# A two-mixture kernel: weight statistics two experts ahead, rows of conditional blocks turned inside the main block, two low parts per expert on GpSimd

## The chip, the cores and the metric

The kernel runs on one core of one Trainium2 chip. The metric is the device time of one execution in microseconds (us); lower is better. Engines are called PE (TensorE matmul), PEld (its weight load), DVE (VectorE), ACT (ScalarE), POOL (GpSimd) and SP (SyncE, which issues most of the transfers).

## The reference

Three layers follow one another on 2304 tokens of width 512: attention inside chunks of 64, a mixture of 8 experts where each token goes to one expert, and a second mixture where each token goes through all 8 experts. Only the first mixture is touched by the change:

```python
logits = x @ w_gate
expert_idx = np.argmax(logits, axis=1)
...
gate_w = probs[np.arange(N), expert_idx]
...
h = np.maximum(np.einsum('ecd,edf->ecf', disp, w1), 0.0)
y = np.einsum('ecf,efd->ecd', h, w2)
...
        out[i] = gate_w[i] * y[expert_idx[i], pos[i]]
```

`disp` holds, for each expert, the tokens that chose it. An expert has a first layer of 512 to 1024 and a second of 1024 to 512, in float32.

## The kernel before

Every float32 matrix is scaled by a power of two and split into two float16 parts, a high one and a low one (the remainder). A product is then three float16 products: high by high, high by low, low by high. The scale of a weight matrix comes from a statistic of the whole matrix.

**Weights of the first mixture.** Expert x has matrix "a" (first layer) and "b" (second). `loads(x, nm)` brings one in as four transfers of 512 KB on SP's queue, into a staging buffer that expert x and expert x + 2 share. `w_stat` takes the statistic of a quarter: for "a" a sum of squares on ACT (line 157), for "b" a maximum on DVE (line 159). `w_scale` adds the quarters up over the partitions with a small PE product, `w_scale2` makes the scale on DVE in some ten tiny operations. `w_split` makes the parts of a quarter: the high part on ACT (line 217), the low part on DVE (line 218) as scale times the staged weights minus the high part. A variant with `on_pool` scales in place on DVE first and subtracts on POOL (line 215); it is used for expert 0 alone, during the attention.

**Tokens of an expert.** `gather` fetches 128 rows at a time by an indirect transfer on POOL's queue (line 652) into one of six `xg` buffers. `turn_dma` transposes the first 256 rows of the next expert by transfers on SP's queue. `turn` transposes on PE instead (line 673): eight 128 by 128 transposes for each 128 rows into a PSUM bank, then one copy on ACT and one on DVE (lines 675 and 676).

**An expert's turn in the loop over x.** `blocks(..., main=True)` computes the first 256 tokens: the first layer in four groups of 24 products (line 705), each followed by `hh` (relu and high part, ACT, line 709) and `hl` (low part, DVE, line 710); then for each 128 tokens t the second layer in 24 products (line 720), its sum of squares on ACT, a scale on DVE, the two halves of the output row (lines 729 and 730) and `rkt`, the token number and the gate factor (lines 735 and 736). The `hh` and `hl` of the main block use PSUM banks "p" (three), the second layer banks "y" (two), the conditional blocks banks "c" (two). Then come the conditional blocks: if the expert has more than 256 tokens, one block of 128, if more than 384, one of 256. With this data experts 0 and 2 run a block of 256, experts 3 and 6 one of 128, experts 1, 4, 5 and 7 none. The rows for the conditional block are `late`; before the change they are turned on PE at the start of the conditional block.

**The order around it.** Each engine takes its instructions in program order. Work on the weights of the next expert y = x + 1 is put into `sites`, six places of the main block of x: after each of the four groups and after each of the two second layers. Before the change the first three sites hold the statistics of y, the fourth its scales and two splits, the fifth four splits, the sixth two. Loads for expert x + 3 follow the main block. Expert 7's sites prepare the first matrix of the second mixture (`w_quad`: sums of sub-blocks on POOL, lines 233 to 236, then parts on ACT and DVE, lines 242 and 243). After the loop the second mixture begins at line 916 with products that read rows already written.

Of the kernel before, what the change touches and what calls it, by code (L numbers as in the profile page):

```python
# [10 lines left out]
F16 = mybir.dt.float16  # L11
# [20 lines left out]
def kernel(ctx, tc, q, k, v, w_gate, w1, w2, capacity, w2_gate, w21, w22, out):  # L32
    nc = tc.nc
# [34 lines left out]
    def sm(nm, shape, dtype=F32):  # L68
        return small_pool[-1].tile(shape, dtype, tag=nm, name=nm)
# [135 lines left out]
        n = 2 * ((x - E) % 2) if x >= E else 2 * (nm == "b")  # L205
        m.hi, m.lo = (w_slot(x, n + i).rearrange("p (k n) -> p k n", n=m.n) for i in range(2))

    def w_split(x, nm, j, nj, on_pool=False):
        m = mats[x, nm]
        c = m.kk // nj  # L210
        sl = slice(j * c, (j + 1) * c)
        if on_pool:
            nc.vector.tensor_scalar(out=m.st[:, sl, :], in0=m.st[:, sl, :], scalar1=m.s, scalar2=None, op0=ALU.mult)
            nc.scalar.copy(out=m.hi[:, sl, :], in_=m.st[:, sl, :])
            nc.gpsimd.tensor_tensor(out=m.lo[:, sl, :], in0=m.st[:, sl, :], in1=m.hi[:, sl, :], op=ALU.subtract)
        else:
            nc.scalar.activation(out=m.hi[:, sl, :], in_=m.st[:, sl, :], func=AF.Copy, scale=m.s)  # L217
            nc.vector.scalar_tensor_tensor(out=m.lo[:, sl, :], in0=m.st[:, sl, :], scalar=m.s, in1=m.hi[:, sl, :],  # L218
                                           op0=ALU.mult, op1=ALU.subtract)
# [44 lines left out]
    with ExitStack() as actx:  # L264
# [310 lines left out]
        def plan(n, f):  # L575
            todo.setdefault(n, []).append(f)

        for nm, ld, st, sc, sp in (("a", (2, 3), (3, 4, 5, 6), 6, (10, 13, 8, 15)), ("b", (9, 10), (11, 10, 12, 12), 12, (15, 14, 16, 13))):
            for h in range(2):
                plan(ld[h], lambda nm=nm, h=h: w_load(0, nm, h))  # L580
                plan(NT + 1, lambda nm=nm, h=h: w_load(1, nm, h))
            for h in range(4):
                plan(st[h], lambda nm=nm, h=h: w_stat(0, nm, h, True))
            plan(sc, lambda nm=nm: (w_scale(0, nm), w_alloc(0, nm)))
            plan(sc + 1, lambda nm=nm: w_scale2(0, nm))
            for h in range(4):
                plan(sp[h], lambda nm=nm, h=h: w_split(0, nm, h, 4, True))

        order = ((st_x1, 4), (st_scale, 5), (st_exp, 3), (st_lo, 6), (st_scores, 2), (st_hi, 5), (st_norm, 4), (st_xtr, 4),
                 (st_max, 2), (st_xcopy, 4), (st_tr, 0), (st_pv, 3), (st_logits, 5), (st_dtr, 2))  # L590
# [46 lines left out]
    with ExitStack() as cctx:  # L637
# [24 lines left out]
            return xT, rows  # L662


        def turn(rows, main):
            if main:
                xT = cp.tile([128, 2 * KD, 256], F16, tag="xT", name="xT", bufs=2)
            else:
                xT = cp.tile([128, 2 * KD, 256], F16, tag="xTc", name="xTc", bufs=1)
            for n, (idx, kg, xg) in enumerate(rows):  # L670
                p = ps_c.tile([128, 2 * KD, 128], F16, tag="y" if main else "c", name="p_t", bufs=2)
                for kk in range(2 * KD):
                    nc.tensor.transpose(p[:, kk, :], xg[:, kk * 128:(kk + 1) * 128], id16)
                sl = slice(n * 128, (n + 1) * 128)
                nc.scalar.copy(out=xT[:, 0:KD, sl], in_=p[:, 0:KD])
                nc.vector.tensor_copy(xT[:, KD:2 * KD, sl], p[:, KD:2 * KD])
            return xT, rows

        def blocks(x, pre, nb, row0, sites=(), main=False):
            a, b = mats[x, "a"], mats[x, "b"]
            xT, rows = pre
            W = 128 * nb
# [2 lines left out]
            def bank(nm, shape):  # L687
                tag, bufs = {"p": ("p", 3), "y": ("y", 2)}[nm] if main else ("c", 2)
                return ps_c.tile(shape, F32, tag=tag, name="p_" + nm, bufs=bufs)

            def site():
                for f in (sites.pop(0) if sites else ()):
                    f()

            hh = cp.tile([128, KF, 256], F16, tag="hh", name="hh", bufs=1)[:, :, 0:W]
            hl = cp.tile([128, KF, 256], F16, tag="hl", name="hl", bufs=1)[:, :, 0:W]
            FG = 512 // W
# [15 lines left out]
            for t in range(nb):  # L713
                idx, kg, _ = rows[t]
                sl = slice(t * 128, t * 128 + 128)
                y = bank("y", [128, DM])
                n = 0
                for kk in range(KF):
                    for h, w in ((hh, b.hi), (hh, b.lo), (hl, b.hi)):
                        nc.tensor.matmul(y, lhsT=h[:, kk, sl], rhs=w[:, kk, :], start=(n == 0), stop=(n == 3 * KF - 1))  # L720
                        n += 1
                sq, ssq = cp.tile([128, DM], BF16, tag="sq", name="sq2", bufs=1), sm("ssq2", [128, 1])
                nc.scalar.activation(out=sq, in_=y, func=AF.Square, accum_out=ssq)
                s, inv = sm("x2s", [128, 1]), sm("x2i", [128, 1])
# [9 lines left out]
                to = sm("rkt", [128, 2])  # L734
                nc.gpsimd.tensor_copy(to[:, 1:2].bitcast(I32), idx)
# [12 lines left out]
        def scales(x):  # L748
            return [lambda f=f, nm=nm: f(x, nm) for f in (w_scale, w_scale2) for nm in "ab"]

        def loads(x, nm, lo=0, hi=4):
            for h in range(lo, hi):
# [19 lines left out]
        late = gather(tokens(0, 2, 3))  # L772
        for f in stats(1):
            f()
        pre = turn(first, True)

        for x in range(E):
            y = x + 1
# [17 lines left out]
            if x == E - 1:  # L796
                with tc.If(rc <= 512):
                    heads()
            if y < E:
                for nm in "ab":  # L800
                    w_alloc(y, nm)
                steps = [stats(y) if x > 0 else []] + [scales(y) + each(w_split, y, "a", 4, 4) + each(w_split, y, "b", 4, 4)]
                counts = (4, 2, 2), (6, 4, 2)
            else:
                w_alloc(E, "a")
                wsums += [xw.tile([128, 4, 2, 128], F32, name=f"wsum{i}") for i in range(2)]
                quads = lambda *qs: [lambda q=q, i=i: w_quad(E, q, i) for q, i in qs]
                steps = [quads((0, 0), (1, 0)) + stats(E),
                         scales(E) + quads((0, 1), (0, 2), (2, 0), (1, 1), (1, 2), (3, 0), (2, 1), (2, 2), (3, 1), (3, 2))]
                counts = (6, 2, 2), (6, 5, 3)  # L810
            sites = []
            for fs, ns in zip(steps, counts):
                for n in ns:
                    sites.append(fs[:n])
                    fs = fs[n:]
                assert not fs
            blocks(x, cur, 2, ranks(0), sites, True)
            if x + 3 < E + 1:
                for nm in "ab":
                    if (x + 3, nm) != (E, "b"):  # L820
                        loads(x + 3, nm)
            if x == E - 2:
                loads(E, "b")
            with tc.If(rc > 256):
                with tc.If(rc > 384) as cmp:
                    blocks(x, turn(late, False), 2, ranks(2))
                    with tc.If(rc > 512):
                        with tc.For_i(4, (rc + 127) // 128, 1) as t:
                            idx = cp.tile([128, 1], I32, tag="idx", name="idx")
                            nc.vector.tensor_copy(idx, gidx[:, x, bass.ds(t, 1)])  # L830
                            blocks(x, turn(gather([idx]), False), 1, lambda _: rank(t))
                        if x == E - 1:
                            heads()
                with cmp.Else():
                    blocks(x, turn(late[:1], False), 1, ranks(2))

    w_alloc(E, "b")
    acctx.close()
# [255 lines left out]
    for x in range(E):  # L1094
# [27 lines left out]
        if x < 2:  # L1122
            for i, f in sq.items():
                if (i >= 34) == (x == 1):
                    plan(2 * (1 - x), i - 34 * x, f)
        if x == 0:
            for h in range(4):
                plan(0, 2 * h + 5, lambda h=h: w_split(E, "b", h, 4))
        for s in range(NSB):
# [73 lines left out]
```

## Time and profile before

| what | us |
|---|---|
| median of 3 runs (1909.0 to 1911.2) | 1910.93 |
| the profiled execution | 1911.24 |
| its span, first to last instruction | 1909.2 |
| the first mixture in it, from the first product of expert 0 (152.49) to the first of the second mixture (455.50) | 303.01 |
| PE busy in this stretch | 254.10 |

The profiled execution lasts 2.04 us longer than its span. Everything that the change edits lies between 152.49 and some microseconds after 455.50.

### The profile page before, as it was taken

To read this page: it belongs to the slowest core of one execution; us is meant where nothing else is said; L and a number is where in the kernel's file an instruction comes from. 1 tells how busy PE (TensorE), PEld (TensorE's weight loads), DVE (VectorE), ACT (ScalarE), POOL (GpSimd) and SP (SyncE) were. 2 spreads that over 40 slices of the span, in tenths; PEclk is the share of its full clock that TensorE was granted. 3 is DMA by queue.
4 is the path that set the end of the run, shared out by engine and by line. 5 is a ranking of instruction groups with operands and counts; after the bars stand their busy time and mean duration, and the time that the engine had idled before them with its cause. 6 is when DMAs were issued, how large, how long until landed. Compare 5 with 4: busy or idle time off the path is not lost.

```text
span 1909.2 us, 27168 instructions
## 1 busy us (share of the span) xinstructions
PE 1789.2 (94%) x10671; PEld 1013.1 (53%) x10671; DVE 1019.8 (53%) x1981; ACT 717.0 (38%) x1300; POOL 404.7 (21%) x470
## 2 busy tenths in 40 slices
PE   6867988888998999999999999999999999999998
PEld 5755645556554445555555555555555555555553
DVE  4894545757656554453555346444535553464432
ACT  7953544646433333332333224322323332242210
POOL 2341101113111211130133014111311230042221
PEclk8987989989999999999999999999999999999999
DMA  9745465754412211121122021311211211212210
GB/s 227 194 156 189 103 231 140 168 152 124 136 42 102 94 59 59 54 93 58 59 102 86 17 102 59 102 59 45 102 59 59 102 67 36 103 58 70 73 42 33
DMA packets 135119, 182.14 MB, mean 95 GB/s; under 512 B 62240, under 2 KB 80752, under 8 KB 134960
## 3 DMA queue, kind: packets, MB, share of 16 engines
q1 hardware_dynamic: 128544, 162.75, 27.3%
q0 software_dynamic: 5360, 17.24, 3.2%
q8 instruction: 100, 1.64, 0.4%
q14 instruction: 59, 0.48, 0.1%
q10 hardware_dynamic: 1056, 0.03, 0.0%
HBM read 149.21 MB, written 23.56 MB: 90 GB/s over the span
## 4 chain that ended last, share of the span: by engine, by line
PE 68%; DVE 4%; ACT 3%; issue 1%; POOL 1%; DMA 0%; POOLq 0%; DVEq 0%
PE p_m L1088 39%; PE p_m L1026 28%; DVE c L1032 1%; DVE el L1043 1%; ACT eh L1042 1%; ACT wsq L157 1%; POOL w L1061 1%; PE p_m L916 0%; PE p_l L166 0%; ACT m L1051 0%; ACT m L1071 0%; DVE w L218 0%; DVE u L1032 0%; ACT w L217 0%; DMA out_dram<-acc,rk 0%
## 5 line engine op out<-in xcount | busy, mean ns | idle before, releaser
L1088 PE MATMUL p_m<-w,eh 128*128 128x512 f16 x2304 | 685.2, 379 | 0.6 <-ACT eh L1042 0.6
L1026 PE MATMUL p_m<-x,w 128*128 128x384 f16 x4032 | 667.6, 327 | 1.3 <-DVE c L1032 1.3
L1026 PEld LDWEIGHTS <-w 128*128 128x128 f16 x4032 | 396.2, 99 | 264.9 <-issue 6.7
L1088 PE MATMUL p_m<-w,el 128*128 128x512 f16 x1152 | 436.6, 379 | 0.0
L1088 PEld LDWEIGHTS <-eh 128*128 128x128 f16 x2304 | 225.4, 98 | 267.7 <-ACT eh L1042 1.1
L1042 ACT ACTIVATE eh<-c 128x384 f16<-128x384 f32 x384 | 190.5, 518 | 413.4 <-DVE c L1032 413.2
L1061 POOL TENSOR_TENSOR w<-u,m 128x384 f32<-128x384 f32 x96 | 96.6, 1006 | 970.3 <-DVE u L1032 913.4
L1160 DVE SCALAR_TENSOR_TENSOR acc<-p_m,cf,acc 128x512 f32<-128x512 f32 x126 | 94.6, 751 | 383.1 <-PE p_m L1088 381.4
L1043 DVE SCALAR_TENSOR_TENSOR el<-c,eh 128x384 f16<-128x384 f32 x384 | 218.0, 569 | 127.0 <-ACT eh L1042 116.4
L1051 ACT COPY m<-p_m 128x384 f32<-128x384 f32 x96 | 44.6, 465 | 399.5 <-PE p_m L1026 399.5
L1088 PEld LDWEIGHTS <-el 128*128 128x128 f16 x1152 | 112.7, 98 | 136.6 <-DVE el L1043 0.8
L705 PEld LDWEIGHTS <-w 128*128 128x128 f16 x1152 | 113.8, 106 | 55.4 <-issue 18.7
L720 PE MATMUL p_y<-w,hh 128*128 128x512 f16 x352 | 105.8, 383 | 0.0
L705 PE MATMUL p_p<-xT,w 128*128 128x256 f16 x768 | 90.9, 282 | 13.8 <-DMA xT<-xg 5.1
L1066 POOL TENSOR_TENSOR c<-u,m 128x384 f32<-128x384 f32 x96 | 95.7, 997 | 3.6 <-DVE u L1032 3.1
L1032 DVE TENSOR_TENSOR u<-p_m,m 128x384 f32<-128x384 f32 x96 | 53.4, 557 | 61.7 <-PE p_m L1026 61.7
L652 POOL DMA_INDIRECT xg<-xs_d,gidx x32 | 37.5, 1171 | 221.6 <-DVE rkt L736 120.5
L1032 DVE TENSOR_TENSOR c<-p_m,w 128x384 f32<-128x384 f32 x96 | 53.5, 558 | 49.2 <-PE p_m L1026 34.4
L218 DVE SCALAR_TENSOR_TENSOR w<-stb,wsb,w 128x1024 f16<-128x1024 f32 x60 | 75.6, 1279 | 7.3 <-ACT w L217 7.2
L1032 DVE TENSOR_TENSOR u<-p_m,u 128x384 f32<-128x384 f32 x96 | 53.5, 557 | 28.7 <-PE p_m L1026 26.9
L157 ACT ACTIVATE wsq<-sta 128x1024 bf16<-128x1024 f32 x64 | 67.4, 1054 | 0.4
L720 PE MATMUL p_y<-w,hl 128*128 128x512 f16 x176 | 67.4, 383 | 0.0
(229 smaller groups left out, 1566.0 us busy)
## 6 DMA issues: line engine op xcount, KB each, us to landing
x<-xt_d SPq DMA_DIRECT2D x147, 384.0 KB, 4.7
sta<-in_moe_w_dram SPq DMA_DIRECT2D x18, 1024.0 KB, 6.0
stb<-in_moe_w_dram SPq DMA_DIRECT2D x18, 1024.0 KB, 7.7
sta<-in_moe_w_dram SPq DMA_DIRECT2D x28, 512.0 KB, 4.6
stb<-in_moe_w_dram SPq DMA_DIRECT2D x28, 512.0 KB, 11.7
xt_d<-x SPq DMA_DIRECT2D x21, 384.0 KB, 3.0
x_d<-row SPq DMA_DIRECT2D x22, 256.0 KB
vbd<-in_v_dram SPq DMA_DIRECT2D x72, 64.0 KB, 4.8
```

Of the source, the lines that this page charges most:

```text
L157: nc.scalar.activation(out=sq, in_=src, func=AF.Square, accum_out=m.mx[:, h:h + 1])
L218: nc.vector.scalar_tensor_tensor(out=m.lo[:, sl, :], in0=m.st[:, sl, :], scalar=m.s, in1=m.hi[:, sl, :], op0=ALU.mult, op1=ALU.subtract)
L705: nc.tensor.matmul(p[:, f4, :], lhsT=w[:, kk, f * 128:(f + 1) * 128], rhs=xT[:, lo + kk, 0:W], start=(n == 0), stop=(n == 3 * KD - 1))
L720: nc.tensor.matmul(y, lhsT=h[:, kk, sl], rhs=w[:, kk, :], start=(n == 0), stop=(n == 3 * KF - 1))
L1026: nc.tensor.matmul(p, lhsT=wt[:, w, lw, kk, :], rhs=xt[:, lx, kk, :], start=(n == 0), stop=(n == 5))
L1032: nc.vector.tensor_tensor(out=c, in0=p, in1=t, op=ALU.add)
L1042: nc.scalar.activation(out=hh[:, sl], in_=src, func=AF.Relu)
L1043: nc.vector.scalar_tensor_tensor(out=hl[:, sl], in0=src, scalar=0.0, in1=hh[:, sl], op0=ALU.max, op1=ALU.subtract)
L1061: nc.gpsimd.tensor_tensor(out=Q["w"], in0=Q["u2"], in1=Q["m5"], op=ALU.add)
L1066: nc.gpsimd.tensor_tensor(out=Q["c22"], in0=Q["u3"], in1=Q["m5"], op=ALU.add)
L1088: nc.tensor.matmul(y, lhsT=h[:, t * 128:(t + 1) * 128], rhs=w[:, kk, :], start=(n == 0), stop=(n == 3 * KF - 1))
L1160: nc.vector.scalar_tensor_tensor(out=acc[:, j, :], in0=y, scalar=coefs[x][:, j:j + 1], in1=acc[:, j, :], op0=ALU.mult, op1=ALU.add)
```

## The change

- Statistics move from expert y = x + 1 to expert x + 2. They stand in one place, after the second layer of t = 0 of the main block, behind the loads for expert x + 3, which move there too (`behind`). For expert 7 this place takes the maxima of matrix "b" of the second mixture; the scale of that matrix is made at the first two steps of the second mixture.
- Scales and splits of y then stand in the first four sites: 4 scale steps and 2 splits, then 2, 2 and 2 splits. `w_quad` of expert 7 stands there too.
- The low parts of quarters 2 and 3 of matrix "b" are made on POOL by two operations: the staged weights times the scale in place, then the subtraction.
- The `late` rows are turned for every expert, between the first and the second layer of the main block (`between`), through two of the banks "p"; always 256 rows, whether the conditional block runs or not.
- The copies of the token numbers (`tos`, POOL) stand at the start of a block and no longer behind its second layers.

```diff
-        if on_pool:
+        if on_pool == 2:
+            nc.scalar.activation(out=m.hi[:, sl, :], in_=m.st[:, sl, :], func=AF.Copy, scale=m.s)
+            nc.gpsimd.tensor_scalar(out=m.st[:, sl, :], in0=m.st[:, sl, :], scalar1=m.s, scalar2=None, op0=ALU.mult)
+            nc.gpsimd.tensor_tensor(out=m.lo[:, sl, :], in0=m.st[:, sl, :], in1=m.hi[:, sl, :], op=ALU.subtract)
+        elif on_pool == 1:
...
+        def turn(rows, tag, bank="y"):
+            xT = cp.tile([128, 2 * KD, 128 * len(rows)], F16, tag=tag, name=tag, bufs=2 if tag == "xT" else 1)
...
+                p = ps_c.tile([128, 2 * KD, 128], F16, tag=bank, name="p_t", bufs=2 if bank != "p" else 3)
...
+            tos = [sm("rkt", [128, 2]) for _ in range(nb)]
+            for (idx, _, _), to in zip(rows, tos):
+                nc.gpsimd.tensor_copy(to[:, 1:2].bitcast(I32), idx)
...
+                if t == 0 and between:
+                    between()
                 y = bank("y", [128, DM])
...
-                steps = [stats(y) if x > 0 else []] + [scales(y) + each(w_split, y, "a", 4, 4) + each(w_split, y, "b", 4, 4)]
-                counts = (4, 2, 2), (6, 4, 2)
+                sp = [lambda h=h, nm=nm: w_split(y, nm, h, 4, 2 * (nm == "b" and h > 1)) for h, nm in
+                      ((0, "a"), (2, "b"), (1, "a"), (2, "a"), (3, "b"), (3, "a"), (0, "b"), (1, "b"))]
+                sc = [lambda f=f, nm=nm: f(y, nm) for f in (w_scale, w_scale2) for nm in "ab"]
+                steps = sc + sp
+                counts = 6, 2, 2, 2
...
-                counts = (6, 2, 2), (6, 5, 3)
+                counts = 6, 3, 3, 2
...
-            blocks(x, cur, 2, ranks(0), sites, True)
...
+            behind = [load_next]
+            for h in range(4):
+                if x + 2 <= E:
+                    behind.append(lambda h=h: w_stat(x + 2, "a", h, True))
+                if x + 2 < E or x == E - 1:
+                    behind.append(lambda h=h: w_stat(min(x + 2, E), "b", h, False))
+            nxt = []
+            sites += [behind, []]
+            blocks(x, cur, 2, ranks(0), sites, True, lambda: nxt.append(turn(late, "xTc", "p")))
+            late_t, late_r = nxt[0]
...
-                    blocks(x, turn(late, False), 2, ranks(2))
+                    blocks(x, (late_t, late_r), 2, ranks(2))
...
-                    blocks(x, turn(late[:1], False), 1, ranks(2))
+                    blocks(x, (late_t, late_r[:1]), 1, ranks(2))
...
         if x == 0:
+            plan(0, 1, lambda: w_scale(E, "b"))
+            plan(0, 2, lambda: w_scale2(E, "b"))
```

## Rows read from the trace of the kernel before

**Rows 1.** First line of the page.
```profile
span 1909.2 us, 27168 instructions
```

**Rows 2.** Windows: stretch, length; PE, PEld, DVE, ACT, POOL busy; PE clock; DMA share, GB/s.
```profile
206.75:229.51 22.76, 21.54 (x149) 14.35 (x148) 16.20 (x32) 14.98 (x23) 3.21 (x5) 1.00 0.52 86
229.51:255.42 25.91, 23.37 (x148) 14.92 (x148) 19.52 (x36) 16.47 (x27) 5.53 (x8) 0.93 0.65 224
...
152.49:455.50 303.01, 254.10 (x1761) 171.60 (x1760) 178.85 (x337) 155.01 (x240) 48.32 (x65) 0.92 0.58 161
```

**Rows 3.** Timeline of PE: start, length, what; in brackets idle before and its releaser.
```profile
241.97 0.39 PE L166 MATMUL p_sum<-wmxa,ones 128*128 128x4 f32 x2 [1.76 <-ACT wsq L157]
...
255.42 1.06 PE L673 MATMUL p_t<-id,xg 128*128 128x128 f16 x16
263.08 13.23 PE L705 MATMUL p_p<-xTc,w 128*128 128x256 f16 x96 [6.61 <-DVE xTc L676]
...
316.50 0.58 PE L705 MATMUL p_p<-xTc,w 128*128 128x128 f16 x4 [5.71 <-ACT xTc L675]
317.84 7.74 PE L705 MATMUL p_p<-xTc,w 128*128 128x128 f16 x92 [0.76 <-DVE xTc L676]
330.60 10.64 PE L705 MATMUL p_p<-xT,w 128*128 128x256 f16 x96
...
383.83 12.59 PE L705 MATMUL p_p<-xT,w 128*128 128x256 f16 x96 [5.08 <-DMA xT<-xg]
...
411.41 0.55 PE L673 MATMUL p_t<-id,xg 128*128 128x128 f16 x6 [4.15 <-issue]
413.30 0.58 PE L705 MATMUL p_p<-xTc,w 128*128 128x128 f16 x4 [1.35 <-ACT xTc L675]
...
455.50 1.65 PE L916 MATMUL p_m<-id,head 128*128 128x128 f16 x14 [7.32 <-DVEq L824]
```

**Rows 4.** Windows: the first 2 us behind the wait at 263.08.
```profile
263.08:265.08 2.00, 2.00 (x10) 1.44 (x11) 0.28 (x1) 0.00 (x0) 0.00 (x0) 0.50 0.63 27
```

**Rows 5.** Lines: group, count, busy us, mean ns, idle before and its releasers.
```profile
L217 ACT ACTIVATE w<-sta,wsa 128x1024 f16<-128x1024 f32 x28 | 30.5, 1139 | 9.0 <-DVE wsa L91 9.0
L218 DVE SCALAR_TENSOR_TENSOR w<-sta,wsa,w 128x1024 f16<-128x1024 f32 x28 | 34.7, 1281 | 3.0 <-ACT w L217 3.0
L709 ACT ACTIVATE hh<-p_p 128x512 f16<-128x512 f32 x44 | 26.2, 595 | 77.8 <-PE p_p L705 70.2 <-issue 4.3 <-DVE row L730 1.6
L710 DVE SCALAR_TENSOR_TENSOR hl<-p_p,hh 128x512 f16<-128x512 f32 x44 | 30.4, 690 | 67.8 <-ACT hh L709 60.5 <-issue 7.1
...
L215 POOL TENSOR_TENSOR w<-stb,w 128x1024 f16<-128x1024 f32 x4 | 8.5, 2131 | 2.2 <-ACT w L214 2.1
L518 POOL TENSOR_SCALAR cols<-iocf,gci 128x144 f16<-128x144 f32 x18 | 11.6, 650 | 5.6 <-DVE gci L506 5.4
```

**Rows 6.** Timeline of ACT, DVE and POOL where splits and POOL's sums lie.
```profile
219.90 2.19 ACT L217 ACTIVATE w<-sta,wsa 128x1024 f16<-128x1024 f32 x2 [1.20 <-DVE wsa L91]
...
440.26 1.15 DVE L243 SCALAR_TENSOR_TENSOR w<-sta,wsa,w 128x512 f16<-128x512 f32 x2
...
639.30 1.61 DVE L243 SCALAR_TENSOR_TENSOR w<-sta,wsa,w 128x512 f16<-128x512 f32 x2
...
639.46 1.17 POOL L233 TENSOR_TENSOR wsum<-sta 128x256 f32<-128x256 f32 x1 [9.83 <-DVE w L243]
```

**Rows 7.** Timeline of POOL: gathers of experts 2 and 3, and expert 7's first sum.
```profile
233.52 2.01 POOL L652 DMA_INDIRECT xg<-xs_d,gidx  x1 [17.01 <-DVE rkt L736]
236.69 0.95 POOL L652 DMA_INDIRECT xg<-xs_d,gidx  x1 [1.15 <-issue]
...
290.26 0.95 POOL L652 DMA_INDIRECT xg<-xs_d,gidx  x1 [27.93 <-issue]
...
431.48 0.74 POOL L233 TENSOR_TENSOR wsum<-sta 128x256 f32<-128x256 f32 x1
```

**Rows 8.** All transfers of the tile `xg`: from issue to landing.
```profile
DMA to landing us min/median/max: 4.2/8.8/11.1
```

More of the change, by code (lines that the diff above doesn't have):

```diff
@@ L206, in w_alloc, with w_split @@
         m.hi, m.lo = (w_slot(x, n + i).rearrange("p (k n) -> p k n", n=m.n) for i in range(2))
-    def w_split(x, nm, j, nj, on_pool=False):
+    def w_split(x, nm, j, nj, on_pool=0):
         m = mats[x, nm]
@@ L586 @@
             for h in range(4):
-                plan(sp[h], lambda nm=nm, h=h: w_split(0, nm, h, 4, True))
+                plan(sp[h], lambda nm=nm, h=h: w_split(0, nm, h, 4, 1))
         order = ((st_x1, 4), (st_scale, 5), (st_exp, 3), (st_lo, 6), (st_scores, 2), (st_hi, 5), (st_norm, 4), (st_xtr, 4),
@@ L662, in turn_dma @@
             return xT, rows
[L665 to L669, printed above, removed]
+        def turn(rows, tag, bank="y"):
+            xT = cp.tile([128, 2 * KD, 128 * len(rows)], F16, tag=tag, name=tag, bufs=2 if tag == "xT" else 1)
             for n, (idx, kg, xg) in enumerate(rows):
-                p = ps_c.tile([128, 2 * KD, 128], F16, tag="y" if main else "c", name="p_t", bufs=2)
+                p = ps_c.tile([128, 2 * KD, 128], F16, tag=bank, name="p_t", bufs=2 if bank != "p" else 3)
                 for kk in range(2 * KD):
@@ L677, in turn, with blocks @@
             return xT, rows
-        def blocks(x, pre, nb, row0, sites=(), main=False):
+        def blocks(x, pre, nb, row0, sites=(), main=False, between=None):
             a, b = mats[x, "a"], mats[x, "b"]
@@ L733, in blocks @@
                                   in_=rhl.rearrange("p c l n -> p (c l n)").bitcast(F32))
-                to = sm("rkt", [128, 2])
-                nc.gpsimd.tensor_copy(to[:, 1:2].bitcast(I32), idx)
+                to = tos[t]
                 nc.vector.scalar_tensor_tensor(out=to[:, 0:1], in0=kg, scalar=inv, in1=iws[x],
@@ L746, in stats @@
             return [f for p in zip(each(w_stat, x, "a", 4, True), each(w_stat, x, "b", 4, False)) for f in p]
-        def scales(x):
-            return [lambda f=f, nm=nm: f(x, nm) for f in (w_scale, w_scale2) for nm in "ab"]
         def loads(x, nm, lo=0, hi=4):
@@ L774 @@
             f()
-        pre = turn(first, True)
+        pre = turn(first, "xT")
         for x in range(E):
@@ L806, with load_next @@
                 wsums += [xw.tile([128, 4, 2, 128], F32, name=f"wsum{i}") for i in range(2)]
-                quads = lambda *qs: [lambda q=q, i=i: w_quad(E, q, i) for q, i in qs]
-                steps = [quads((0, 0), (1, 0)) + stats(E),
-                         scales(E) + quads((0, 1), (0, 2), (2, 0), (1, 1), (1, 2), (3, 0), (2, 1), (2, 2), (3, 1), (3, 2))]
-                counts = (6, 2, 2), (6, 5, 3)
+                steps = [lambda f=f: f(E, "a") for f in (w_scale, w_scale2)] + [
+                    lambda q=q, i=i: w_quad(E, q, i) for q, i in ((0, 0), (1, 0), (0, 1), (0, 2), (2, 0), (1, 1), (1, 2),
+                                                                  (3, 0), (2, 1), (2, 2), (3, 1), (3, 2))]
+                counts = 6, 3, 3, 2
             sites = []
[L812 to L816, printed above, removed]
-            blocks(x, cur, 2, ranks(0), sites, True)
-            if x + 3 < E + 1:
+            for n in counts:
+                sites.append(steps[:n])
+                steps = steps[n:]
+            assert not steps
+            def load_next():
                 for nm in "ab":
-                    if (x + 3, nm) != (E, "b"):
+                    if x + 3 <= E and (x + 3, nm) != (E, "b"):
                         loads(x + 3, nm)
-            if x == E - 2:
-                loads(E, "b")
+                if x == E - 2:
+                    loads(E, "b")
+            behind = [load_next]
[8 more added lines that the diff above has]
+            late_t, late_r = nxt[0]
             with tc.If(rc > 256):
                 with tc.If(rc > 384) as cmp:
-                    blocks(x, turn(late, False), 2, ranks(2))
+                    blocks(x, (late_t, late_r), 2, ranks(2))
                     with tc.If(rc > 512):
@@ L830 @@
                             nc.vector.tensor_copy(idx, gidx[:, x, bass.ds(t, 1)])
-                            blocks(x, turn(gather([idx]), False), 1, lambda _: rank(t))
+                            blocks(x, turn(gather([idx]), "xTl", "c"), 1, lambda _: rank(t))
                         if x == E - 1:
```

## The prediction

> **What bounds the kernel now.** I read the windows first [rows 2]. The first mixture takes 303.01 us, and PE is busy in 254.10 of them; the mean granted clock is 0.92. So some 49 us of waiting and a slow clock can be won here at most, and nothing outside is edited. A main block without trouble takes 22.76 us (expert 1). Expert 2's takes 25.91, with the same number of products.
>
> PE's timeline shows where the rest goes [rows 3]. Ahead of a conditional block PE makes the transposes and then waits until DVE has copied them: 6.61 us at 263.08 (and the same at expert 0), 5.71 and 0.76 at expert 3, 1.35 and again 0.76 at expert 6. DVE and ACT are not slow there; they still have splits of the next expert in front of the copies. At 241.97 PE waits for the statistics of expert 3, at 383.83 for transposed rows that came by transfer, at 455.50 for DVE, which is still splitting.
>
> A wait costs twice. Behind the one at 263.08 the granted clock is 0.50 [rows 4], the lower of the two levels (1.2 GHz against 2.4), and the 96 products take 13.23 us where they take 10.64 at the full clock [rows 3]. Behind the 5.08 us wait they take 12.59.
>
> **What the change removes.** The sum is made against the profiled execution, 1911.24 us (span 1909.2 [rows 1] and 2.04 around it), 0.31 above the median of the runs.
>
> 1. The late rows are turned some 10 us before they are needed, so the copies are hidden by the second layers. Removed: 6.61 twice, 6.47, and 1.35 + 0.76 = 2.11 [rows 3]: 21.8 us. The 4.15 us "issue" at expert 6 is no wait for data; I leave it in place.
> 2. The slow clock behind them: 13.23 - 10.64 = 2.6 for expert 2 and 1.9 for each of the others, by the other slow run of 96 products (12.59 - 10.64): 8.3. Against it, DVE reaches the conditional block's first `hl` later relative to PE than before; an estimate of 0.7 each: -2.8.
> 3. Statistics two experts ahead: expert 2's wait goes, with the clock behind it. 25.91 - 22.76 [rows 2], the same work: 3.2.
> 4. Loads leave the queue some 6 us earlier (behind t = 0 and not behind t = 1: one second layer with its tail, (22.76 - 10.64)/2), so the gathers of the next expert meet fewer of them, and expert 6's rows arrive in time: 5.08 and 1.95 of clock, 7.0.
> 5. At the end of expert 7 no splits are left behind its last product. What stays is the row's own tail: for expert 1 `rkt` released the gather at 233.52 [rows 7], 4.0 behind the end of its block at 229.51 [rows 2]. 7.32 - 4.0: 3.3.
>
> Gains: 21.8 + 8.3 - 2.8 + 3.2 + 7.0 + 3.3 = 40.8.
>
> **What it adds.**
>
> 6. Transposes: 8 experts with 16 make 128 where there were 48. 80 by 1.06/16 [rows 3]: 5.3 on PE. The two copies on ACT and DVE lie under the second layers.
> 7. The second of the two banks that `turn` takes is the third group's: PE, at 10.64 + 0.5 = 11.2 us of the block, waits until `hl` of the third group has read it. On ACT the first `hh` (0.60 [rows 5]) follows the first group at 10.64/4 = 2.7, and the splits begin 1.20 behind it, when the scale is there (the wait at 219.90 [rows 6]): 4.5. Then come two splits (2.19 for two [rows 6]), `hh`, two splits: 9.5. DVE ends the second low part 1.28 later, at 10.8, and `hl` (0.69) at 11.5, up to 11.9 with the hand-overs. So PE waits 0.3 to 0.7 where nothing else interferes; I take 0.7 for experts 0, 1, 3 and 4: 2.8.
> 8. The transposes wait for the late rows themselves. The second gather of an expert is issued only when the block in front is over. Behind a conditional block it goes at 290.26, 2.4 us into expert 3: landing 4.2 to 11.1 later [rows 7, 8], 6.6 to 13.5, mostly hidden by the 10.7 us before the transposes. Behind a main block alone it also waits for `rkt`: at 236.69, 7.2 into expert 2, landing at 11.4 to 18.3. That is 0.7 to 7.6 of wait. The median (8.8) would give 5.3; since the weights' loads are ahead of it now, I take 4, and 1.5 for the clock, at experts 2 and 5, and 2 at expert 6, in front of which only half the loads are issued early: 13.0.
> 9. Expert 7's sums start on POOL 4.7 us in (431.48 [rows 7]), and its splits, which follow them, now stand in front of `hl`: 4.0.
> 10. The subtraction in two operations on POOL. DVE is rid of two of 1.281 per expert [rows 5]. POOL's `TENSOR_TENSOR` of this size takes 2.131; its scaling of 1024 columns has no row. It can't be cheaper than 0.65 (144 columns) nor dearer than 650 x 1024/144 = 4.6 [rows 5]; I take 1.9, nearer the operation of the same width. POOL has room: 5.53 us busy of 25.91 [rows 2], and the low part of "b" is wanted only in the next expert's second layer. The cost is elsewhere: at 639.30 a pair on DVE took 1.61 where it takes 1.15, and POOL's sum that began beside it 1.17 where it takes 0.74 [rows 6, 7]: each lost about 0.45 to the other. Behind four gathers POOL begins some 7 to 13 us into the block, when most of DVE's early splits are past. I count one collision per block as hidden, since DVE saves 2.6.
> 11. The copies of `tos` and the scale of "b" in the second mixture: nothing. The copies run behind the gathers as before; nobody but POOL's own splits queues behind them. The scale's small operations, moved into the second mixture, would cost about the 1.20 that ACT waits for one [rows 6] if its start had no cover. On SP the loads now stand in front of the second row's writes and of the next expert's `turn_dma`, and they wait for the staging buffer, so for POOL's low parts too: by item 10 these end some 8 us behind their start (two times 1.9 + 2.131), about when the first second layer does, and `turn_dma` waits for later gathers anyway. Without that cover the next main block starts late, by what the low parts overrun.
>
> For 10, the Trainium skill, SBUF — State Buffer, "SBUF: two separate sides", says that a GpSimd operation and a DVE operation with two SBUF inputs exclude one another for a whole instruction. The trace agrees at 639.30. By that rule a DVE split could lose up to a whole POOL operation, which speaks against this part of the change; the rival below prices it from rows.
>
> Costs: 5.3 + 2.8 + 13.0 + 4.0 = 25.1. Net: 40.8 - 25.1 = 15.7 less. 1911.24 - 15.7 = 1895.5; I say **1896 us**.
>
> **The rivals.**
>
> *A, slower: POOL's operations hold DVE back in front of `hl`.* If both low parts that precede the third `hl` meet a POOL operation of 2.131 in full, `hl` comes 4.3 later, PE waits 4.3 more in each of 7 experts, with the clock's price at some: 30 us, 1926. It decides from 2.2 us per block on (15.7 / 7), one whole operation each time. For it: rows 6. Against it: POOL's place behind the gathers, and that DVE is busy 16.20 of 22.76 us, a part of it on PSUM. Chance 0.12.
>
> *B, no more than the present: late rows are late everywhere.* With landings at 11.1, experts 2 and 5 wait 3.6 more each, 6 some 4, and experts 1, 3, 4 and 7 each 2.1 more (13.5 - 10.7 - 0.7): 20 us at most, 1915; at half of it 1905. For it: the transfers were already late at 383.83. Against it: earlier loads. Chance 0.16, centre 1905.
>
> *C, all hidden.* Items 8 and 9 cost nothing, only transposes and short waits remain: 15.7 + 17 = 32.7 us less, 1879. It needs gathers that land in 4.2 us with no loads beside them. Chance 0.14.
>
> *D, nothing gained:* a main block becomes longer by what the conditional one loses, since ACT and DVE have as much to do as before. With 16.20 and 14.98 of 22.76 us busy [rows 2] they are not full; the same work moves under PE's. Chance 0.04, 1911.
>
> **How the numbers follow.** My forecast has 0.54; its own range is 1885 to 1908 (item 8 by its ends: three times 0.7 without the clock, three times 7.6 with it). The range that leaves out 2 in 10: C's upper half below, B's lower half above, and some of the unpriced scaling in 10: 1881 to 1910. What a measurement of this kernel can tell from no change is about 0.2%, 3.8 us. Forecast and C lie below 1907.1; B half below, a third within, the rest above; D within; A above. Faster 0.76, same 0.10, slower 0.14.
>
> **What would show it.** In the changed kernel's timeline of PE: no wait for `xTc` copies ahead of conditional blocks, and their first 96 products in some 10.7 us; sixteen transposes between first and second layer of every expert, with waits for the gather of several us at experts 2 and 5 and below 1 at the others; no wait for `wsq` or `wmxb`; some 4 us ahead of line 916. Products of a main block plus transposes should take 23 to 24 us. On POOL two operations of about 2 us per quarter; `hl` of the third group by 12 us. I am wrong if PE's waits at the transposes exceed some 35 us together, whether DVE (A) or the gather (B) ends them, or if DVE's splits are longer than 1.3 us throughout.

## The result and the profile after

The changed kernel takes 1888.99 us (median of 4 runs, 1884.21 to 1895.42), the one before 1911.07 in the same comparison: ratio 0.989 [0.986, 0.992]. It is faster, by some 22 us where 15 were forecast. The profiled execution of the changed kernel is the longest of its runs, 1895.42 us, 15.8 below the profiled one before; a repeat later (below) had a median of 1886.01. So the rows of this section show somewhat more waiting than an ordinary run has.

The windows of the changed kernel, columns as in [rows 2]: experts 2 (main and conditional block), 6 (both) and 7, then the whole first mixture.

```profile
224.12:248.86 24.74, 22.59 (x164) 15.40 (x164) 19.16 (x37) 18.62 (x29) 7.16 (x7) 1.00 0.74 231
248.86:271.07 22.21, 21.13 (x145) 14.05 (x144) 8.14 (x19) 7.57 (x16) 8.41 (x7) 1.00 0.74 244
...
355.86:402.31 46.45, 37.99 (x285) 26.12 (x284) 18.84 (x41) 20.79 (x33) 22.02 (x15) 0.85 0.59 150
402.31:438.05 35.74, 25.18 (x163) 16.02 (x162) 25.14 (x41) 15.87 (x27) 16.85 (x19) 0.85 0.24 76
...
154.11:438.05 283.94, 252.49 (x1838) 171.16 (x1838) 178.34 (x327) 159.50 (x250) 126.51 (x93) 0.95 0.62 171
```

The first mixture is 19.07 shorter (303.01 before [rows 2]). In this pair of executions 1.62 of it are lost ahead of expert 0's first product and 1.95 behind the first mixture; the repeat has neither loss. PE's busy time fell by 1.6 only, although it makes 80 transposes more; the rest of the gain, 17.5, is waiting that is gone. Measured with the same windows in both kernels, the four conditional blocks became 29.9 shorter together, and the eight main blocks 10.9 longer: expert 7's by 7.05, expert 6's by 5.17, expert 4's by 2.37, while expert 5's became 4.24 shorter and expert 2's 1.17.

Of expert 5's 4.24, some is in no item of the prediction. Before, PE stands for 2.92 in the middle of expert 5's first layer and waits for nothing that the profile shows ("issue"); the 83 products behind it take 10.88, where 9.2 would do at the full clock (83/96 of 10.64). Neither is there in the changed kernel. The row of before:

```profile
357.15 10.88 PE L705 MATMUL p_p<-xT,w 128*128 128x256 f16 x83 [2.92 <-issue]
```

PE's timeline of the changed kernel, the rows that answer to [rows 3]:

```profile
236.36 0.62 PE L674 MATMUL p_t<-id,xg 128*128 128x128 f16 x8 [0.72 <-DMA xg<-xs_d,gidx]
238.06 0.61 PE L674 MATMUL p_t<-id,xg 128*128 128x128 f16 x8 [1.08 <-DVE hl L714]
248.86 10.77 PE L709 MATMUL p_p<-xTc,w 128*128 128x256 f16 x96
...
293.42 5.52 PE L709 MATMUL p_p<-xTc,w 128*128 128x128 f16 x96
...
355.86 2.78 PE L709 MATMUL p_p<-xT,w 128*128 128x256 f16 x24 [1.64 <-DMA xT<-xg]
368.67 0.62 PE L674 MATMUL p_t<-id,xg 128*128 128x128 f16 x8 [1.80 <-DMA xg<-xs_d,gidx]
370.63 1.03 PE L674 MATMUL p_t<-id,xg 128*128 128x128 f16 x8 [1.34 <-DMA xg<-xs_d,gidx]
392.22 5.07 PE L709 MATMUL p_p<-xTc,w 128*128 128x128 f16 x50 [5.31 <-issue]
...
413.88 0.61 PE L674 MATMUL p_t<-id,xg 128*128 128x128 f16 x8 [0.78 <-DVE hl L714]
418.22 1.01 PE L674 MATMUL p_t<-id,xg 128*128 128x128 f16 x8 [3.74 <-DVE hl L714]
438.05 1.68 PE L931 MATMUL p_m<-id,head 128*128 128x128 f16 x14 [6.03 <-SPq L839]
```

The conditional blocks of experts 2 and 3 start without a wait, and their 96 products take 10.77 and 5.52 us, the time at the full clock. The wait for statistics at expert 2 is gone. What came instead stands at the transposes: gathers that land late, and `hl` that comes late. The largest, 3.74 at expert 7, has the lower clock behind it. Windows of the 2 us that follow:

```profile
418.22:420.22 2.00, 2.00 (x11) 1.25 (x11) 2.00 (x3) 1.35 (x2) 1.92 (x3) 0.50 0.00 0
```

The groups of instructions of the first mixture, one row for each shape:

```profile
L214 POOL TENSOR_SCALAR stb<-stb,wsb 128x1024 f32<-128x1024 f32 x14 | 44.9, 3204 | 7.8 <-ACT w L213 7.8
L222 DVE SCALAR_TENSOR_TENSOR w<-sta,wsa,w 128x1024 f16<-128x1024 f32 x28 | 36.7, 1330 | 7.9 <-ACT w L221 7.9
...
L222 DVE SCALAR_TENSOR_TENSOR w<-stb,wsb,w 128x1024 f16<-128x1024 f32 x14 | 24.5, 1790 | 0.0
...
L674 PE MATMUL p_t<-id,xg 128*128 128x128 f16 x128 | 10.6, 230 | 13.0 <-DMA xg<-xs_d,gidx 6.6 <-DVE hl L714 5.6 <-DVE w L222 0.6
```

The last row sums up all the waits at transposes: 13.0 us. The prediction called itself wrong from some 35 on. The splits of "b" that are left on DVE take 1.79 instead of 1.28, beside POOL's operations.

### The profile page after: what moved, and what is told of

Its sections match the earlier page's. It is cut to its first block, busy times and chain, and to the rows that moved or that the text cites. A ratio compares the mean times of both kernels' runs of the same rounds, so it can differ in the third digit from the quotient of the medians.

```text
span 1893.7 us, 27401 instructions
## 1 busy us (share of the span) xinstructions
PE 1792.2 (95%) x10751; PEld 1016.1 (54%) x10751; DVE 1020.1 (54%) x1977; ACT 721.6 (38%) x1310; POOL 483.3 (26%) x498
## 4 chain that ended last, share of the span: by engine, by line
PE 68%; DVE 4%; ACT 3%; issue 1%; POOL 1%; DMA 0%; POOLq 0%; DVEq 0%
PE p_m L1103 39%; PE p_m L1041 28%; DVE c L1047 1%; DVE el L1058 1%; ACT eh L1057 1%; ACT wsq L157 1%; POOL w L1076 1%; PE p_l L166 0%; PE p_m L931 0%; ACT m L1066 0%; DVE u L1047 0%; ACT m L1086 0%; DVE w L222 0%; ACT w L221 0%; DMA out_dram<-acc,rk 0%
## 5 line engine op out<-in xcount | busy, mean ns | idle before, releaser
L1041 PEld LDWEIGHTS <-w 128*128 128x128 f16 x4032 | 396.5, 99 | 266.2 <-issue 8.6
L709 PEld LDWEIGHTS <-w 128*128 128x128 f16 x1152 | 107.9, 101 | 27.1 <-issue 12.6
L246 ACT ACTIVATE w<-wsum,wsa 128x1024 f16<-128x1024 f32 x32 | 36.7, 1146 | 85.8 <-POOL wsum L240 85.8
L222 DVE SCALAR_TENSOR_TENSOR w<-stb,wsb,w 128x1024 f16<-128x1024 f32 x46 | 65.4, 1433 | 6.2 <-ACT w L221 6.1
```

Of the source, the lines that this page charges most:

```text
L709: nc.tensor.matmul(p[:, f4, :], lhsT=w[:, kk, f * 128:(f + 1) * 128], rhs=xT[:, lo + kk, 0:W], start=(n == 0), stop=(n == 3 * KD - 1))
L1041: nc.tensor.matmul(p, lhsT=wt[:, w, lw, kk, :], rhs=xt[:, lx, kk, :], start=(n == 0), stop=(n == 5))
```

## The experiments

Ten kernels, in three batches; a ratio is always to the kernel before, run in the same batch (1908.04, 1909.15 and 1909.29 us). The first batch has 1 to 4, the second 5 to 8, the third 9 and 10.

**1. No low part on POOL.**

```diff
-w_split(y, nm, h, 4, 2 * (nm == "b" and h > 1))
+w_split(y, nm, h, 4, 0)
```

> The changed kernel with the low parts of quarters 2 and 3 of "b" back on DVE in one operation each. Theory (the two POOL operations are about neutral: what DVE saves in two splits of 1.28 us it loses to POOL's operations beside it): within 4 us of the changed kernel's 1889, stretch of the first mixture 280 to 288 us against 283.9. Rival (they cost: the DVE splits that remain last 1.79 us in the mean for "b", and expert 6's gathers queue behind POOL's splits): 5 to 12 us faster, stretch 272 to 279. Other rival (they pay, DVE being the bound): 5 us or more slower.

Measured 1885.99 us, 0.9886 [0.9871, 0.9900]; the changed kernel itself, repeated in the second batch, has 0.9881 [0.9866, 0.9897]. Its groups:

```profile
L222 DVE SCALAR_TENSOR_TENSOR w<-stb,wsb,w 128x1024 f16<-128x1024 f32 x28 | 35.2, 1279 | 0.0
...
L674 PE MATMUL p_t<-id,xg 128*128 128x128 f16 x128 | 10.1, 224 | 9.1 <-DVE hl L714 9.1
```

DVE's splits are back at 1.28 us, but there are twice as many of "b", and `hl` still comes late: 9.1 us of waits for it. No transpose waits for a gather here. The first mixture takes 274.77 in this profile, as the rival said; but experiment 5, with POOL's part, has 276.54, so that is no sign for it. POOL's part neither gives nor costs time that can be measured.

**2. The late rows turned at the conditional blocks again**, all the rest of the change kept.

```diff
-blocks(x, cur, 2, ranks(0), sites, True, lambda: nxt.append(turn(late, "xTc", "p")))
+blocks(x, cur, 2, ranks(0), sites, True)
...
-blocks(x, (late_t, late_r), 2, ranks(2))
+blocks(x, turn(late, "xTc", "c"), 2, ranks(2))
...
```

> The changed kernel, but the late rows are turned at the start of a conditional block again, and only where one runs. Theory (the 22 us of waits ahead of conditional blocks go because the rows are turned earlier): the waits come back at 2 to 6 us at each of the four blocks, with a slow clock where they are long; the eight turns in the main blocks and their waits go (17 us with their clock); the stretch 280 to 295 us, so no more than 4 us of gain and up to 11 of loss. Rival (they go because the splits now stand earlier, so the copies find DVE and ACT free): each wait under 2 us, the stretch 262 to 272, and 1870 to 1878 in all.

Measured 1896.94 us, 0.9939 [0.9927, 0.9951]. PE's timeline has waits for the copies again, 15.6 us at the four blocks where it was 21.8 before, and the slow products behind them too:

```profile
180.47 12.15 PE L709 MATMUL p_p<-xTc,w 128*128 128x256 f16 x96 [3.70 <-DVE xTc L677]
...
254.20 6.05 PE L709 MATMUL p_p<-xTc,w 128*128 128x256 f16 x34 [5.85 <-DVE xTc L677]
```

So most of these waits go with the turn, and some 6 us of them with the rest of the change alone.

**3. Only the turn inside the main block**, the statistics, splits and low parts as before.

```diff
...
-blocks(x, cur, 2, ranks(0), sites, True)
+nxt = []
+blocks(x, cur, 2, ranks(0), sites, True, lambda: nxt.append(turn(late, "xTc", "p")))
+late_t, late_r = nxt[0]
...
```

> The kernel before with one part of the change: the late rows of every expert are turned between first and second layer, statistics, splits and copies of token numbers stay in their old places and on their old engines. Theory (this part carries most of the gain): 30 us of waits and slow clock at conditional blocks go, 5 us of transposes come, and gathers are late at experts 2, 5 and 6 by 2 to 7 us each; 1892 to 1902. Rival (the order of statistics and splits carries it): under 6 us of gain, 1905 to 1913, because the copies, the statistics and the splits crowd the second layers.

Measured 1892.75 us, 0.9925 [0.9912, 0.9939]. PE's timeline:

```profile
182.68 5.40 PE L702 MATMUL p_p<-xTc,w 128*128 128x256 f16 x48 [2.53 <-DVE hl L707]
...
234.99 0.39 PE L166 MATMUL p_sum<-wmxa,ones 128*128 128x4 f32 x2 [1.76 <-ACT wsq L157]
236.15 0.39 PE L166 MATMUL p_sum<-wmxb,ones 128*128 128x4 f32 x2 [0.78 <-DVE wmxb L159]
```

The turn alone gives 15.3 us (1908.04 - 1892.75), the rest of the change without it 11.1 (experiment 2). Both together gave 23.1 (1909.15 - 1886.01), 3.3 less than the sum; with intervals of 2 to 3 us on each side, that they overlap is not shown. The first row shows why the turn alone is not the whole: DVE's splits that once delayed the copies now delay the first `hl` of the conditional block by 2.53; with the splits moved forward that wait is gone.

**4. Expert 7's preparation spread.** The four maxima of matrix "b" of the second mixture stand between the parts of "a" in the first layer of the main block, and the last five of the twelve steps of `w_quad` (one of sums, four of parts) move behind the first second layer.

```diff
-counts = 6, 3, 3, 2
+mb = [lambda h=h: w_stat(E, "b", h, False) for h in range(4)]
+steps = (steps[:5] + [mb[0]] + [steps[5], mb[1]] + [steps[6], mb[2], mb[3]] + steps[7:9] + steps[9:])
+counts = 6, 2, 3, 2, 5
...
-if x + 2 < E or x == E - 1:
-    behind.append(lambda h=h: w_stat(min(x + 2, E), "b", h, False))
+if x + 2 < E:
+    behind.append(lambda h=h: w_stat(x + 2, "b", h, False))
...
```

> The changed kernel with expert 7's work spread again over the first layer and the first second layer: the maxima of the second mixture's "b" after groups 1 to 3 and not behind the first second layer, half of the sums' parts behind it. Theory (expert 7's block is 35.7 us and not 28.7 because its parts hold up the reads of two banks ahead of the transposes, 4.5 us of wait and 2 of slow clock, and the maxima stand in front of the last row): the block takes 27 to 30 us, the whole 6 to 8 less than the changed kernel, 1881 to 1883. Rival (the block's length is the work of DVE and POOL, whatever its order): 34 to 37 us, no change.

Measured 1878.05 us, 0.9848 [0.9834, 0.9862]. The window of expert 7 and its only wait in the middle:

```profile
390.90:420.82 29.92, 22.19 (x163) 15.07 (x161) 21.60 (x41) 15.54 (x27) 13.91 (x19) 0.98 0.28 90
```

```profile
403.59 0.61 PE L674 MATMUL p_t<-id,xg 128*128 128x128 f16 x8 [1.47 <-DVE hl L714]
420.82 1.68 PE L933 MATMUL p_m<-id,head 128*128 128x128 f16 x14 [6.27 <-SPq L841]
```

29.92 us instead of 35.74, and PE busy for 22.19 instead of 25.18, with as much work: the difference of the busy times is the clock (0.98 against 0.85). The waits at the transposes fall from 4.52 to 1.47. These two are the whole of the 5.82; the end is no shorter (6.27 against 6.03), so moving the maxima away from the last row shows no gain there.

**5. The changed kernel again**, unchanged.

> The changed kernel once more, beside the three below on one chip, since its profiled execution (1895) lay 6 us above its median (1889). Theory (the difference is the gathers, which land now earlier, now later): 1884 to 1893, the same blocks within 1 us, but for experts 5 and 6, where the waits for rows and for code add up differently. Rival (a steady cost of 9 us against the kernel without POOL's low parts): 1893 or more.

Measured 1886.01 us (1881.45 to 1887.64), 0.9881 [0.9866, 0.9897]; its first mixture takes 276.54 us in the profile, which was taken in the shortest of its runs. The waits at the transposes are 10.0 instead of 13.0, and expert 6 takes 43.03 instead of 46.45. What the first profile shows above that is variation from run to run, at experts 2 and 4 too (1.1 and 1.3).

**6. Turned inside the main block only for the experts that run a conditional block with this data** (0, 2, 3, 6); for the others no rows are turned.

```diff
-blocks(x, cur, 2, ranks(0), sites, True, lambda: nxt.append(turn(late, "xTc", "p")))
+blocks(x, cur, 2, ranks(0), sites, True, (lambda: nxt.append(turn(late, "xTc", "p"))) if x in (0, 2, 3, 6) else None)
...
```

> The changed kernel, but the late rows of experts 1, 4, 5 and 7, whose conditional blocks do not run with this data, are not turned in the main block. Theory (a turn there costs PE 1.1 to 1.3 us and what PE waits for the gather or for a bank): 4 times 1.2, 1.3 at expert 4, 2 at expert 5, 2 to 6 at expert 7: 7 to 13 us less than the changed kernel beside it. Rival (the waits only move on, into the second layer, because ACT and DVE set the pace of a main block): 3 us or less.

Measured 1886.24 us, 0.9872 [0.9850, 0.9893]: no difference, as the rival said. Where the transposes are left out, something else is late. PE's timeline at the start of expert 6 and in the second layer of expert 7:

```profile
351.92 5.28 PE L709 MATMUL p_p<-xT,w 128*128 128x256 f16 x24 [3.77 <-DMA xT<-xg]
...
411.58 0.39 PE L726 MATMUL p_y<-w,hl 128*128 128x512 f16 x1 [1.41 <-DVE hl L714]
```

Expert 6's rows come 3.77 late (1.60 in experiment 5), and 24 products then take 5.28 for 2.78. In expert 7 the wait for `hl` moves from the transposes into the second layer.

**7. The copies of the token numbers behind the second layers again.**

```diff
-            tos = [sm("rkt", [128, 2]) for _ in range(nb)]
-            for (idx, _, _), to in zip(rows, tos):
-                nc.gpsimd.tensor_copy(to[:, 1:2].bitcast(I32), idx)
...
-                to = tos[t]
+                to = sm("rkt", [128, 2])
+                nc.gpsimd.tensor_copy(to[:, 1:2].bitcast(I32), idx)
```

It was made for these rows of POOL's timeline in the changed kernel:

```profile
351.29 0.31 POOL L698 COPY rkt<-gidx 128x1 int32<-128x1 int32 x2 [11.80 <-DMA rk_d<-rkt]
351.58 2.85 POOL L214 TENSOR_SCALAR stb<-stb,wsb 128x1024 f32<-128x1024 f32 x1
354.51 2.13 POOL L215 TENSOR_TENSOR w<-stb,w 128x1024 f16<-128x1024 f32 x1
...
364.07 1.03 POOL L656 DMA_INDIRECT xg<-xs_d,gidx  x1 [2.39 <-DVE w L222]
...
368.48 0.95 POOL L656 DMA_INDIRECT xg<-xs_d,gidx  x1 [0.30 <-issue]
```

A copy of 0.31 us reuses a buffer whose write to memory must have landed, and waits 11.80 for it. Behind it on POOL stand four operations of 10.1 us, and behind these the gathers, four of them from 364.07, 8.2 us into expert 6's block (2.39 of it after POOL is free, released by DVE). The transposes of 368.67 and 370.63 wait for them.

> The changed kernel with the copies of the token numbers back behind the second layers. Theory (their place is of no weight to the time): within 3 us of the changed kernel beside it. Rival 1 (at the block's start they wait up to 12 us for the landing of older token numbers and hold POOL's low parts and so the next gathers back; without them POOL is done sooner): 4 to 8 us less, and the waits for the gather at the transposes, 7 us in all, under 3. Rival 2 (behind the second layers they stand behind POOL's low parts, and the last row of a block is late): 3 us or more slower.

Measured 1881.49 us, 0.9858 [0.9843, 0.9873]; POOL's timeline and the group of the transposes:

```profile
343.39 0.30 POOL L738 COPY rkt<-gidx 128x1 int32<-128x1 int32 x2
351.08 1.02 POOL L656 DMA_INDIRECT xg<-xs_d,gidx  x1 [7.38 <-DVEq L837]
```

```profile
L674 PE MATMUL p_t<-id,xg 128*128 128x128 f16 x128 | 10.1, 224 | 8.1 <-DVE hl L711 7.9
```

The copy waits for nothing now, the gather is issued 2.8 us into the block (348.30 to 351.08), and no transpose waits for a gather. The waiting is shown; the gain of 4.5 us beside experiment 5 is not sure by this pair, for the two intervals overlap.

**8. The spread of 4, and no low part on POOL.**

> The changed kernel with both of the first two useful edits: expert 7's work spread as before, and all low parts on DVE. Theory (the first is worth 7 to 8, the second nothing in the median, so together 7 to 8): 1877 to 1882. Rival (both are worth something, the second 5 or more): 1869 to 1874.

Measured 1877.68 us, 0.9845 [0.9830, 0.9859]. That is 8.3 us below experiment 5 of the same batch, the intervals lie apart, and by experiment 4 POOL's part is again worth nothing.

**9. The spread of 4 and the copies of 7 together.**

> Expert 7's preparation spread over the block and the copies of the token numbers put back behind the second layers, together. Theory: the two act at different places (the end of expert 7; POOL's queue in front of the gathers of experts 5 and 6), so their gains of about 8 and 4.5 us add up: 1872 to 1876 us, no wait of PE's transposes for a gather and an end of expert 7 as in the kernel with the spread alone. Rival: the gain of 4.5 was variation between runs or lies at expert 7 as well; then the time stays at that of the spread alone, 1877 to 1880 us.

Measured 1876.79 us (1874.67 to 1883.06), 0.9825 [0.9812, 0.9839]. Among the kernels run it has the lowest ratio. The median lies between the two expectations, 1.3 below that of experiment 4, which ran in another batch; by the ratios to the kernel before it is 0.0023 lower (4.4 us), as much as 7 is below 5. The intervals overlap here too, so these runs do not decide whether the two gains add up. The profiled execution is its longest. Its window of expert 6, the rows of DVE and POOL in it, and PE's:

```profile
349.45:396.24 46.79, 38.48 (x285) 26.67 (x285) 21.40 (x40) 20.87 (x33) 18.92 (x12) 0.85 0.51 149
```

```profile
359.67 4.35 DVE L222 SCALAR_TENSOR_TENSOR w<-sta,wsa,w 128x1024 f16<-128x1024 f32 x2 [0.35 <-ACT w L221]
363.94 0.68 DVE L711 SCALAR_TENSOR_TENSOR hl<-p_p,hh 128x512 f16<-128x512 f32 x1
```

```profile
360.40 2.54 POOL L215 TENSOR_TENSOR w<-stb,w 128x1024 f16<-128x1024 f32 x1
362.92 3.81 POOL L214 TENSOR_SCALAR stb<-stb,wsb 128x1024 f32<-128x1024 f32 x1
```

```profile
364.67 1.01 PE L674 MATMUL p_t<-id,xg 128*128 128x128 f16 x8 [3.77 <-DVE hl L711]
```

With the gathers early, POOL's low parts are early too, and meet DVE's splits: two take 4.35 us for 2.56, POOL's own 2.54 and 3.81 for 2.13 and 2.85. `hl` stands behind the pair, and PE waits 3.77, then runs at the lower clock.

**10. The same without low parts on POOL.**

> The same, and all low parts on DVE. Theory: with the copies of the token numbers behind the second layers POOL's low parts hold up no gather any more, so taking them away changes nothing or costs a little, since DVE has two more splits per expert: equal to the kernel with both edits within 2 us. Rival: POOL's operations still lengthen DVE's splits at a place that matters; then it is 3 us or more faster.

Measured 1878.17 us, 0.9832 [0.9819, 0.9846]: no difference, as expected. In its profile the wait at the same place is 1.80:

```profile
362.13 0.61 PE L674 MATMUL p_t<-id,xg 128*128 128x128 f16 x8 [1.80 <-DVE hl L711]
```

So the collision costs 2.0 there (3.77 - 1.80) and the clock behind it; expert 6 takes 42.30 in place of 46.79. Expert 7 takes longer without POOL's part, 31.73 in place of 29.85, because the second mixture starts later:

```profile
422.91 1.68 PE L931 MATMUL p_m<-id,head 128*128 128x128 f16 x14 [8.09 <-SPq L839]
```

All three profiles without POOL's part have this longer end (7.84, 7.92 and 8.09; the other kernels with the new order have 5.24 to 6.27). It lies behind the last `rkt`, not in DVE's or POOL's work, and its cause was not looked for. So "nothing" for POOL's part may hide a gain in the blocks of up to 2 us that this end takes back.

## Why the prediction was right, and where its terms were off

The direction and the cause were right; 1888.99 is 7 below the 1896 and in the range. The forecast's own sum has two halves. The conditional blocks should become shorter by 21.8 + 8.3 - 2.8 and the 48 transposes that leave them (3.2), 30.5; they became 29.9 shorter. The main blocks should become 14.8 longer (the costs of 25.1 and these 3.2, less 13.5 by items 3 to 5); they became 10.9 longer in the profile shown. The first mixture of the repeat is 7.4 shorter still, so its costs were smaller again.

That both halves come out so near is in part luck. In the main blocks 4.6 (2.92 and 1.7 of clock) are expert 5's "issue" wait, which no item has; without it they would be 15.5 longer. And there errors of both signs meet: items 4 and 5 gave 3.6 less than forecast, items 6 and 9 cost 5.6 more, items 7 and 8 cost less.

- **Items 1 and 2, waits and clock at the conditional blocks:** held. The products run at 10.77 and 5.52 us, and experiment 2 brings waits and slow products back. The "issue" at expert 6, which I left in place, is there: 5.31. With the clock behind it (50 products in 5.07, 2.95 in experiment 4) it is why that block became only 1.70 shorter. The 2.8 taken off for a late first `hl` were not needed: PE's waits for `hl` in these blocks are 0.38 here, 1.10 in the repeat.
- **Item 3, statistics:** held. Expert 2's block takes 24.74 and 1.3 of it are its new transposes, 1.80 the waits there; the waits for `wsq` and `wmxb` still stand in experiment 3, which has the old order of the statistics.
- **Item 4, expert 6's rows:** the wait fell from 5.08 to 1.64 and the clock behind it is full (24 products in 2.78): 5.4 of the 7.0. That the earlier loads did it is not shown: experiment 3 has the loads in their old place, and there PE does not wait for these rows at all, but 1.16 for a split:

```profile
366.32 10.64 PE L702 MATMUL p_p<-xT,w 128*128 128x256 f16 x96 [1.16 <-ACT w L217]
```

- **Item 5, the end of expert 7:** 1.3 in place of 3.3. `rkt` ends 4.05 behind the last product (432.02 to 436.07), near the 4.0 of the sum, but by luck: the row's statistic is ready on ACT at 432.80, and DVE begins the scale only at 434.11, behind the maxima that the change put there. And I took the 4.0 from a case where POOL's gather follows `rkt`; here SP has to issue the row's write first, and PE starts 1.98 later. In experiment 4, where four parts stand in front of the last row and no maxima, the end is 6.27 too.

These are DVE's, ACT's and SP's rows at the end of expert 7, then DVE's in its middle, of the changed kernel:

```profile
429.60 4.59 DVE L159 TENSOR_REDUCE wmxb<-stb 128x1 f32<-128x1024 f32 x4
434.11 0.14 DVE L90 TENSOR_SCALAR x2h<-ssq 128x1 int32<-128x1 int32 x1
...
435.86 0.21 DVE L741 SCALAR_TENSOR_TENSOR rkt<-xg,x2i,iw 128x1 f32<-128x1 f32 x1
```

```profile
432.61 0.19 ACT L729 ACTIVATION_READ_ACCUMULATOR sq<-p_y 128x1 f32 x1
```

```profile
436.92 0.34 SPq L743 DMA_DIRECT2D rk_d<-rkt  x1
```

```profile
413.14 0.68 DVE L714 SCALAR_TENSOR_TENSOR hl<-p_p,hh 128x512 f16<-128x512 f32 x1
413.75 2.16 DVE L247 SCALAR_TENSOR_TENSOR w<-sta,wsa,w 128x512 f16<-128x512 f32 x2
415.83 1.74 DVE L247 SCALAR_TENSOR_TENSOR w<-wsum,wsa,w 128x1024 f16<-128x1024 f32 x1
417.49 0.68 DVE L714 SCALAR_TENSOR_TENSOR hl<-p_p,hh 128x512 f16<-128x512 f32 x1
```

- **Item 9, expert 7's splits in front of `hl`:** the wait was sized well, 4.0 against 0.78 + 3.74. What I left out is the clock behind it, though the prediction says itself that a wait costs twice: expert 7's PE is busy 3.0 longer than in experiment 4. Expert 7 is the largest loss of the change, and the only edit that got a large part back is the one that spreads its work: 5.8 us in its window, and by the ratios 6.3 and 7.8 in the whole time (4 against 5, 8 against 1).
- **Item 6, transposes:** 128, as said. They take 10.6 us, some at the lower clock, where 48 took 3.2: 7.4 against 5.3.
- **Items 7 and 8, `hl` and gathers at the transposes:** priced too dear, the largest error on that side. Without expert 7 the waits come to 8.5 us in the profile shown (13.0 - 4.5) and 5.5 in the repeat, against 12.8 (2.8, and 10.0 of the 13.0). At expert 2 the gather is 0.72 late and at expert 5 1.40, not 4. At expert 6 it is later than I said (3.14 against 2, and the clock), for a reason that I had put at nothing: item 11.
- **Item 11, the copies:** "nobody but POOL's own splits queues behind them" is wrong. Through the splits, the next expert's gathers do. Experiment 7 shows the chain. Its price in time is less sure: three pairs differ in the copies' place alone (7 and 5, 9 and 4, 10 and 8), and the ratio is lower behind the second layers in each, by 0.0023, 0.0023 and 0.0013 (4.4, 4.4 and 2.5 us); in no pair do the intervals lie apart.
- **Item 10, low parts on POOL:** nothing, as taken, in three pairs (1 and 5, 8 and 4, 10 and 9). Its sizes were off: the scaling takes 2.85 us uncontended, not 1.9, and collisions are longer than the one of 0.45 that I counted (the splits of "b" lose 0.51 each). My sign "longer than 1.3 us throughout" was half there, and the time was not hurt. The Trainium skill, SBUF — State Buffer, "SBUF: two separate sides", has a DVE operation with two SBUF inputs and a GpSimd operation that reads SBUF exclude one another for a whole instruction. The pair in experiment 9, which lost 1.79 beside an operation of 2.13, agrees with that.
- **The rivals:** A (POOL holds DVE back) is real at one place in one profile, 2.0 us at expert 6 in experiment 9, and not in every block, where it would have had to be 2.2. B (late rows everywhere) did not happen: at expert 4 a gather was 1.34 late once, and at 1, 3 and 7 none. C (all hidden, 1879) is nearer than I gave it; the kernels with expert 7 spread reach its time. D fell: the main blocks take back 10.9 of the 29.9.

Three things stay open. The "issue" wait in expert 6's conditional block is between 1.09 and 5.78 us over the kernels and was not pursued. While it lasts, one packet of an instruction queue is moved in the kernel before, the changed one and the repeat, as in expert 5's wait before, so PE may be waiting for its code; no run tests that. Whether the gains of 4 and 7 add up is not decided: by the ratios they do, and the collision that stands against it is seen in one execution (experiment 9's profile). And of the 11.1 us that the rest of the change gives without the turn (experiment 2), the statistics, the place of the splits and the earlier loads were not run one by one.

## What to carry to other kernels

Work that only reads data already there, such as transposes, belongs in front of other products of PE, so that the copies behind it are hidden; it frees the wait and the slow clock behind the wait, and both were worth 15 us here (experiment 3) with the total of PE's work increased. When other work is moved into the same block, price it by what stands behind it in its engine's queue, up to the next gather, and price every wait with the clock that follows. A small instruction that waits for a transfer to land should not stand in a queue in front of the issue of the next transfers.

## What was not expected of the hardware

- POOL's scaling of 128x1024 float32 in place takes 2.85 us, longer than its subtraction of two tensors of that size, 2.13.
- DVE and POOL lengthen each other by more than was seen before: a pair of splits 4.35 for 2.56, POOL's scaling 3.81 for 2.85. Over the first mixture of the changed kernel DVE's splits are 8.5 us longer by it (28 by 0.05 and 14 by 0.51), and no difference to the time could be measured.
- A copy of 0.31 us on POOL stood for 11.80 us, until a write of token numbers had landed.
